# An attention with two mixtures of experts: first products by seven block products, second products in two groups, and an order set by a list scheduler

## The chip, the cores and the metric
The kernel runs on one core of a Trainium2 chip. The metric is the device time of one execution in microseconds; a median of several executions is compared. All inputs lie in the chip's memory at the start, and the output is written there.

## The reference
Local and pooled attention over 576 tokens (2 batches, 8 heads of 64) gives 1152 tokens of 512 values. A mixture of 8 experts, whose weights come from a gate normalized in 8 rounds over rows and columns, makes new tokens of them, and a second mixture of 4 experts, with given probabilities, makes the output.
```python
# attention: exp of scores less their maxima, windows of 7 keys, plus means over 4 tokens
x = attn_out.transpose(0, 2, 1, 3).reshape(1152, 512)
# first mixture: w1 (8, 512, 1024), w2 (8, 1024, 512)
P = np.exp(x @ w_gate - (x @ w_gate).max())
for _ in range(8):
    P /= P.sum(1, keepdims=True) + 1e-09
    P /= P.sum(0, keepdims=True) + 1e-09
    P *= N / E
for e in range(E):
    h = np.maximum(x @ w1[e], 0.0)
    out += P[:, e:e + 1] * (h @ w2[e])
# second mixture: the same with 4 experts on out, and p = domain_probs / their sums
```

## The kernel before
Every operand of a product is kept as two parts of the type fp32r, a high part (a rounded copy) and a low part (the rest). A product is three matmuls: high by high, high by low, low by high. Tokens are split like this in `xh` and `xl`, the hidden activations in `hh` and `hl`, the weights in `w1h`, `w1l`, `w2h`, `w2l`.

The attention goes over 8 pairs of heads (4 in each batch of 576 tokens) in a hand-written order. From pair 4 on, units of the first expert's first products for batch 0 (`filler`, 288 tokens by 128 hidden values, 12 matmuls) stand between its steps. The gate of the first mixture follows, its 8 rounds interleaved with the same units for batch 1.

Then the experts come one after the other. For the first products (`p1_in`, L128) an expert takes 8 tiles `f` of hidden values and 3 blocks of 384 tokens, 12 matmuls each (4 slices of the model dimension, three parts). `p1_out` makes the high part on ACT (L148) and the low part on DVE (L150). For the second products (`p2_in`, L164) it takes 9 tiles of 128 tokens, 24 matmuls of 512 columns each; `p2_out` scales them with the expert's probability and adds them into `acc` on DVE (L181). Weights are loaded in pieces of 128x512 into a ring of four buffers (`load_next`, SP's queue), and `split` makes the high part on ACT (L116) and the low part on POOL (L117), one piece per unit of products. Behind expert 7 `turn` transposes the result into new `xh` and `xl`. The order of all engines is the order in which the code is written.

## Time and profile before
| what | value |
|---|---|
| three runs | 1283.47, 1284.67 and 1288.3 us, median 1284.67 us |
| span of the profiled execution | 1281.9 us (its own time is not listed apart; 1.6 us below the quickest run) |
| busy: TensorE, weight loads, DVE, ACT, POOL | 1273.6, 1157.3, 319.6, 314.9, 289.4 us |
| chain that ended last, first and second products | 47% and 46% of the span |
| HBM traffic | 60.0 MB read, 49 GB/s |

The busy times of all engines overlap. A matmul's busy time includes its way through the array, so the distance between the starts of two matmuls in a row is what one costs. The chain of work that ended last is followed back from the last instruction to what released it.

### The profile page before, as it was taken

Reading aid. Unit: us, or ns where it says so; the run is one execution under the profiler, and the core shown is the slowest. Engines: PE = TensorE matmul, PEld = TensorE weight load, DVE = VectorE, ACT = ScalarE, POOL = GpSimd, SP = SyncE. Lnnn points to the kernel's source line nnn. Section 1 sums busy time; section 2 is a strip of 40 time slices with the busy share of each in tenths; the row PEclk is TensorE's granted clock in tenths of the full one; section 3 lists DMA queues with packets and bytes.
Section 4 is the critical chain, followed back from the end, with each engine's and each line's share of the span. In section 5 each row is a group of like instructions: output and inputs, shape, how many; then the busy total and the mean of one; then the engine's idle time right before and its main releaser. Section 6 shows DMA issues by size and latency. Waiting matters only on the chain.

```text
span 1281.9 us, 17529 instructions
## 1 busy us (share of the span) xinstructions
PE 1273.6 (99%) x7166; PEld 1157.3 (90%) x7166; DVE 319.6 (25%) x681; ACT 314.9 (25%) x758; POOL 289.4 (23%) x245
## 2 busy tenths in 40 slices
PE   9899999999999999999999999999999999999998
PEld 8799889889889989989989989989988988988987
DVE  6855202112112212212212212222200211211211
ACT  3653223203203303302302302312322320320310
POOL 5742222302402401401401311211221230230210
PEclk9899999999999999999999999999999999999999
DMA  7421111201301301200200210110111120120101
GB/s 199 137 64 48 54 38 43 89 1 42 91 1 36 97 1 34 84 16 27 81 25 25 63 45 22 46 49 25 46 45 42 42 82 1 47 86 1 34 26 50
DMA packets 33761, 63.52 MB, mean 50 GB/s; under 512 B 5280, under 2 KB 6048, under 8 KB 33680
## 3 DMA queue, kind: packets, MB, share of 16 engines
q1 hardware_dynamic: 33680, 62.40, 16.8%
q8 instruction: 56, 0.92, 0.3%
q14 instruction: 25, 0.20, 0.0%
HBM read 60.02 MB, written 2.36 MB: 49 GB/s over the span
## 4 chain that ended last, share of the span: by engine, by line
PE 97%; DVE 1%; ACT 0%; DMA 0%; issue 0%; ACTq 0%
PE bank L128 47%; PE bank L164 46%; PE bank L293 1%; PE bank L456 0%; PE bank L334 0%; PE bank L431 0%; DVE xl L491 0%; PE bank L192 0%; ACT ed L370 0%; DVE ed L400 0%; PE bank L739 0%; DMA qk<-in_qk_dram 0%; PE bank L464 0%; DVE mxd L348 0%; DVE sm L318 0%; PE bank L286 0%
## 5 line engine op out<-in xcount | busy, mean ns | idle before, releaser
L128 PE MATMUL bank<-xh,w1h 128*128 128x384 f32 (+1 forms) x1184 | 392.9, 332 | 0.0
L128 PE MATMUL bank<-xl,w1h 128*128 128x384 f32 (+1 forms) x1184 | 391.1, 330 | 0.0
L128 PE MATMUL bank<-xh,w1l 128*128 128x384 f32 (+1 forms) x1184 | 391.0, 330 | 0.0
L164 PE MATMUL bank<-w2h,hh 128*128 128x512 f32 (+1 forms) x872 | 339.9, 390 | 0.0
L164 PE MATMUL bank<-w2h,hl 128*128 128x512 f32 (+1 forms) x872 | 339.8, 390 | 0.0
L164 PE MATMUL bank<-w2l,hh 128*128 128x512 f32 (+1 forms) x872 | 337.4, 387 | 0.0
L148 ACT ACTIVATE hh<-bank 128x384 fp32r<-128x384 f32 (+5 forms) x392 | 148.9, 405 | 720.2 <-PE bank L128 685.9
L117 POOL TENSOR_TENSOR w2l<-stg,w2h 128x512 fp32r<-128x512 f32 x96 | 124.2, 1294 | 794.5 <-ACT w2h L116 794.5
L150 DVE SCALAR_TENSOR_TENSOR hl<-bank,hh 128x384 fp32r<-128x384 f32 (+5 forms) x392 | 168.1, 449 | 512.4 <-ACT hh L148 512.0
L128 PEld LDWEIGHTS bank<-xh,w1h 128*128 128x128 f32 x1184 | 222.8, 188 | 1.2 <-DVE sm L318 0.4
L128 PEld LDWEIGHTS bank<-xl,w1h 128*128 128x128 f32 x1184 | 222.9, 188 | 0.4
L128 PEld LDWEIGHTS bank<-xh,w1l 128*128 128x128 f32 x1184 | 222.8, 188 | 0.0
L164 PEld LDWEIGHTS bank<-w2l,hh 128*128 128x128 f32 x872 | 163.7, 188 | 34.9
L164 PEld LDWEIGHTS bank<-w2h,hh 128*128 128x128 f32 x872 | 163.8, 188 | 34.9
L164 PEld LDWEIGHTS bank<-w2h,hl 128*128 128x128 f32 x872 | 163.9, 188 | 32.1
L181 DVE SCALAR_TENSOR_TENSOR acc<-bank,prob,acc 128x512 f32<-128x512 f32 (+1 forms) x91 | 67.8, 745 | 416.7 <-PE bank L164 416.7
L117 POOL TENSOR_TENSOR w1l<-stg,w1h 128x512 fp32r<-128x512 f32 x96 | 122.6, 1300 | 115.9 <-ACT w1h L116 115.0
L116 ACT ACTIVATE w1h<-stg 128x512 fp32r<-128x512 f32 x96 | 58.2, 628 | 46.0 <-DMA stg<-in_w1a_dram 32.6
L116 ACT ACTIVATE w2h<-stg 128x512 fp32r<-128x512 f32 x96 | 59.8, 623 | 0.0
L179 ACT ACTIVATE acc<-bank,prob 128x512 f32<-128x512 f32 x18 | 12.4, 689 | 78.2 <-PE bank L164 66.4
L293 PEld LDWEIGHTS bank<-qk 64*64 64x64 f32 x288 | 21.2, 172 | 4.0 <-issue 2.9
L293 PE MATMUL bank<-qk 64*64 64x70 f32 x288 | 24.0, 271 | 0.2 <-DMA qk<-in_qk_dram 0.2
(94 smaller groups left out, 315.2 us busy)
## 6 DMA issues: line engine op xcount, KB each, us to landing
stg<-in_w1a_dram SPq DMA_DIRECT2D x64, 256.0 KB
stg<-in_w2a_dram SPq DMA_DIRECT2D x64, 256.0 KB
stg<-in_w1b_dram SPq DMA_DIRECT2D x32, 256.0 KB
stg<-in_w2b_dram SPq DMA_DIRECT2D x32, 256.0 KB
qk<-in_qk_dram SPq DMA_DIRECT2D x7, 576.0 KB
vw<-in_vw_dram SPq DMA_DIRECT2D x8, 315.0 KB
v<-in_v_dram SPq DMA_DIRECT2D x8, 288.0 KB
out_dram<-acc SPq DMA_DIRECT2D x8, 256.0 KB
```

Of the source, the lines that this page charges most:

```text
L116: nc.scalar.activation(out=hi, in_=t, func=ACTF.Copy)
L117: nc.gpsimd.tensor_tensor(out=lo, in0=t, in1=hi.bitcast(F32), op=ALU.subtract)
L128: nc.tensor.matmul(out=ps[:, 0:n], lhsT=a[f][:, k, :], rhs=b[:, k, t0:t0 + n], start=(k == 0 and p == 0), stop=(k == HP - 1 and p == 2),)
L148: nc.scalar.activation(out=hi, in_=ps[:, s:s + m], func=ACTF.Relu)
L150: nc.vector.scalar_tensor_tensor(out=lo, in0=ps[:, s:s + m], scalar=0.0, in1=hi.bitcast(F32), op0=ALU.max, op1=ALU.subtract,)
L164: nc.tensor.matmul(out=ps[:, 0:nd], lhsT=a[k][:, c:c + 128], rhs=b[k][:, c0:c0 + nd], start=(k == 0 and p == 0), stop=(k == NF - 1 and p = ...
L179: nc.scalar.activation(out=a, in_=ps, func=ACTF.Copy, scale=s)
L181: nc.vector.scalar_tensor_tensor(out=a, in0=ps, scalar=s, in1=a, op0=ALU.mult, op1=ALU.add)
L293: nc.tensor.matmul(out=sc[p0:p0 + 64, (t - lo) * W:(t - lo + 1) * W], lhsT=qk_t[p0:p0 + 64, 0, 64 * t:64 * t + 64], rhs=qk_t[p0:p0 + 64, 1 ...
```

## The change
The first products are made by Strassen's scheme. The two batches of 576 tokens and the two halves of the model dimension are the 2x2 blocks of one operand, the halves of the model dimension and two tiles of hidden values (`q` and `q` + 4, a *quarter*, 256 values) the blocks of the other. Seven products per quarter stand in place of eight: products 1, 2 and 4 use blocks of x, products 5, 6, 7 and 3 use sums of its blocks (`sh`, `sl`, made once per mixture by `x_sums` with POOL, DVE and ACT). Each product is made for two halves `u` of 288 tokens, 6 matmuls of 288 columns. `quad` makes the weights of the seven products, with four differences on POOL and seven splits. `quarter_products` puts the seven together in three pairs of banks, with additions on DVE and POOL in SBUF tensors (`p1`, `p5`, `u2`), from which `hidden` makes the parts of the activations.

The second products come after every two quarters (a *group*): nine tiles of 12 matmuls, with an accumulation each, so an expert has two. The hidden activations of one group (`ht`) are kept, not of a whole expert. The first group of experts 0 and 8 has its first products plain, in units of 288 tokens. In expert 0 the probability is multiplied in at the end.

All of it behind the attention is handed to `Plan` as tasks with an engine, a cost and what they read and write. `run` sets the order on each engine: of the first 48 tasks of an engine it takes the one that can begin first by its costs, with tasks of the gate ahead of all. In the attention the fillers are 8 units of first products and 8 halves of second products, and the loads for them go through `raw1` (one buffer of 128x1024) and `raw2` (two).

```diff
+class Plan:
+    AFTER = {"PE": 260.0, "ACT": 120.0, "DVE": 120.0, "POOL": 140.0, "DMA": 0.0}
+    LOOK = 48
...
+        def start(i):
+            e, cost, _, deps, bufs, _ = T[i]
+            t = free[e]
+            for d in deps:
+                if not done[d]:
+                    return None
+                t = max(t, end[d] + (0.0 if T[d][0] == e else self.AFTER[T[d][0]]))
...
+                if b.at != b.ring.given:
+                    return None
+                s = b.ring.free()
+                if s is None:
+                    return None
+                t = max(t, s[0] + 150.0)
+            return t
...
+    def load_first(j):
+        if j < 2:
+            nc.sync.dma_start(out=raw1[0].rearrange("p a b -> p (a b)"), in_=w1a[0, j])
...
+    def split_first(j):
+        if j < 4:
+            q, h = divmod(j, 2)
+            for b in (2 * h, 2 * h + 1):
+                t, w = raw1[0][:, b], w1s[4 * q + b]
+                nc.scalar.activation(out=w[:, 0], in_=t, func=ACTF.Copy)
+                nc.gpsimd.tensor_tensor(out=w[:, 1], in0=t, in1=w[:, 0].bitcast(F32), op=ALU.subtract)
+            if j == 1:
+                load_first(1)
...
-    nsplit = {3: 1, 4: 2, 5: 2, 6: 2, 7: 1}
+    nsplit = {3: 1, 4: 2, 5: 3, 6: 2}
...
+    raw1.append(late.tile([128, 4, 256], F32, name="raw1_1"))
...
+    r_w1, r_w2, r_raw1, r_raw2 = Ring(w1s), Ring(w2s), Ring(raw1), Ring(raw2)
+    r_t = Ring([late.tile([128, 256], F32, name=f"t_{j}") for j in range(3)])
+    r_tmp = Ring([late.tile([128, U], F32, name=f"tmp_{j}") for j in range(8)])
...
+    def split(ring, src, key, n):
+        b = ring.new()
+        plan.add("ACT", copy_cost(n), lambda: nc.scalar.activation(
+            out=b.slot[:, 0], in_=src(), func=ACTF.Copy), (key,), ((b, 0),))
+        plan.add("POOL", pool_cost(n), lambda: nc.gpsimd.tensor_tensor(
+            out=b.slot[:, 1], in0=src(), in1=b.slot[:, 0].bitcast(F32), op=ALU.subtract),
+            (key, (b, 0)), ((b, 1),))
+        return b
...
+    def quad(g, q):
+        r = load_quad(g, q)
...
+        def less(x, kx, y, ky):
+            t = r_t.new()
+            plan.add("POOL", pool_cost(256), lambda: nc.gpsimd.tensor_tensor(
+                out=t.slot, in0=x(), in1=y(), op=ALU.subtract), (kx, ky), (t,))
+            return lambda: t.slot, t
+        w = {1: split(r_w1, b11, r, 256)}
+        t1, k1 = less(b12, r, b11, r)
+        w[5] = split(r_w1, t1, k1, 256)
+        t2, k2 = less(b22, r, t1, k1)
+        w[6] = split(r_w1, t2, k2, 256)
+        w[2] = split(r_w1, b21, r, 256)
+        t3, k3 = less(b22, r, b12, r)
+        w[7] = split(r_w1, t3, k3, 256)
+        w[3] = split(r_w1, b22, r, 256)
+        t4, k4 = less(b21, r, t2, k2)
+        w[4] = split(r_w1, t4, k4, 256)
+        return w
...
+    def product(p, w, ps, u, first):
...
+            o = ps.slot[:, 0:U]
+            for k in range(2):
+                for n, (j, hl) in enumerate(((0, 0), (0, 1), (1, 0))):
+                    if kind == "x":
+                        c = i * S + u * U
+                        a = (xh, xl)[hl][:, rest[0] + k, c:c + U]
+                    else:
+                        a = (sh, sl)[hl][:, i, k, u * U:u * U + U]
+                    nc.tensor.matmul(
+                        out=o, lhsT=w.slot[:, j, 128 * k:128 * k + 128], rhs=a,
+                        start=(first and k == 0 and n == 0), stop=(k == 1 and n == 2),
+                        skip_group_check=True,
+                    )
+        plan.add("PE", 6 * 133.4, fn, [(w, 0), (w, 1), *keys], (ps,))
...
+    def add(dst, ps, b, cost=457.0):
+        plan.add("DVE", cost, lambda: nc.vector.tensor_tensor(
+            out=dst.slot, in0=ps.slot[:, 0:U], in1=b.slot, op=ALU.add), (ps, b), (dst,))
+    def quarter_products(w, q):
+        fa, fb = 2 * (q % 2), 2 * (q % 2) + 1
+        R = range(2)
+        X, p1 = [r_bank.new() for u in R], [r_tmp.new() for u in R]
+        for u in R:
+            product(1, w[1], X[u], u, True)
+            act_copy(lambda u=u: p1[u].slot, lambda u=u: X[u].slot[:, 0:U], 412.0, (X[u],), (p1[u],))
+        Z, p5 = [r_bank.new() for u in R], [r_tmp.new() for u in R]
+        for u in R:
+            product(5, w[5], Z[u], u, True)
+            act_copy(lambda u=u: p5[u].slot, lambda u=u: Z[u].slot[:, 0:U], 412.0, (Z[u],), (p5[u],))
+            plan.add("POOL", pool_cost(U), lambda u=u: nc.gpsimd.tensor_tensor(
+                out=p5[u].slot, in0=p5[u].slot, in1=p1[u].slot, op=ALU.add), (p1[u], p5[u]), (p5[u],))
+        Y, u2 = [r_bank.new() for u in R], [r_tmp.new() for u in R]
+        for u in R:
+            product(6, w[6], Y[u], u, True)
+            add(u2[u], Y[u], p1[u])
+        for u in R:
+            product(2, w[2], X[u], u, False)
+            hidden(lambda u=u: X[u].slot[:, 0:U], X[u], fa, 0, u, P_EVICT)
+        for u in R:
+            product(7, w[7], Y[u], u, False)
+            add(p5[u], Y[u], p5[u])
+            hidden(lambda u=u: p5[u].slot, p5[u], fb, 1, u, S_EVICT)
+        for u in R:
+            product(3, w[3], Z[u], u, False)
+            add(u2[u], Z[u], u2[u])
+            hidden(lambda u=u: u2[u].slot, u2[u], fb, 0, u, S_EVICT)
+        for u in R:
+            product(4, w[4], Y[u], u, False)
+            add(p1[u], Y[u], p1[u])
+            hidden(lambda u=u: p1[u].slot, p1[u], fa, 1, u, S_EVICT)
...
+    def x_sums(j):
...
+                t = part[b][h]
+                plan.add("POOL", pool_cost(2 * wd), lambda t=t, o=o, h=h: nc.gpsimd.tensor_tensor(
+                    out=v(t), in0=xh[:, 2 * h:2 * h + 2, o:o + wd].bitcast(F32),
+                    in1=xl[:, 2 * h:2 * h + 2, o:o + wd].bitcast(F32), op=ALU.add), keys, (t,))
+        def two(dst, x, y, op):
+            plan.add("DVE", dve_cost(2 * wd), lambda: nc.vector.tensor_tensor(
+                out=v(dst), in0=v(x), in1=v(y), op=op), (x, y), (dst,))
+        (a11, a12), (a21, a22) = part
+        two(a22, a21, a22, ALU.add)
+        two(a21, a11, a21, ALU.subtract)
+        two(a11, a22, a11, ALU.subtract)
+        two(a12, a12, a11, ALU.subtract)
+        for i, t in enumerate((a22, a11, a21, a12)):
+            hi, lo = sh[:, i, :, c:c + wd], sl[:, i, :, c:c + wd]
+            plan.add("ACT", copy_cost(2 * wd), lambda t=t, hi=hi: nc.scalar.activation(
+                out=hi, in_=v(t), func=ACTF.Copy), (t,), (("s", i, j, 0),))
+            plan.add("DVE", dve_cost(2 * wd), lambda t=t, hi=hi, lo=lo: nc.vector.tensor_tensor(
+                out=lo, in0=v(t), in1=hi.bitcast(F32), op=ALU.subtract),
+                (t, ("s", i, j, 0)), (("s", i, j, 1),))
...
+    def gate_round(it):
+        pc = r_bank.new()
+        gate("PE", 600.0, lambda: nc.tensor.matmul(
+            out=pc.slot[:, 0:ncol], lhsT=ones, rhs=prob1.rearrange("p n e -> p (n e)")), ("p",), (pc,))
...
+    first_w1 = [held(r_w1, j) for j in range(8)]
+    first_w2 = [held(r_w2, j) for j in range(4)]
+    gate_start()
+    plan.later = [(9000.0 + 4200.0 * it, lambda it=it: gate_round(it)) for it in range(8)]
+    for q in range(2):
+        for h in range(2):
+            for u in range(2):
+                plain_unit(first_w1[4 * q + 2 * h:4 * q + 2 * h + 2], 2 * q + h, 1, u)
+        for j in range(2):
+            x_sums(2 * q + j)
+    for n in range(4, NN):
+        accumulate(0, n, tile_products(first_w2, n), "copy")
+    for q in (2, 3):
+        quarter_products(quad(0, q), q)
+    w2_ = second(0, 1)
...
-    for g in range(NE):
-        last1 = g == E1 - 1
-        if g:
-            for f in range(NF):
-                for j, (t0, n) in enumerate(blocks):
...
-                    p1_group(f, t0, n)
-                split(g, 1, f)
...
+    for g in range(1, NE):
+        for grp in range(2):
+            if g == E1 and grp == 0:
+                ws = [plain_quad(g, q) for q in range(2)]
+                for b, u in T_OF:
+                    for q in range(2):
+                        for h in range(2):
+                            plain_unit(ws[q][2 * h:2 * h + 2], 2 * q + h, b, u)
+                            if (b, u, q, h) == (0, 0, 0, 1):
+                                turn(NN - 1)
+                for j in range(4):
+                    x_sums(j)
...
```

**TensorE in a later expert.** Before, two parts of one block of tokens (`w1h_102` and `w1l_110` are the weights of hidden tile 4; columns 384):
```order
L128 MATMUL bank_119<-xh,w1h_102 128x384
L128 MATMUL bank_119<-xl,w1h_102 128x384
L128 MATMUL bank_119<-xh,w1l_110 128x384
L128 MATMUL bank_119<-xh,w1h_102 128x384
L128 MATMUL bank_119<-xl,w1h_102 128x384
L128 MATMUL bank_119<-xh,w1l_110 128x384
```
Now, product 1 for both halves and the first matmuls of product 5 (`w1s_80`, `w1s_81` hold high and low part):
```order
L900 MATMUL bank_105<-xh,w1s_80 128x288
L900 MATMUL bank_105<-xl,w1s_80 128x288
L900 MATMUL bank_105<-xh,w1s_80 128x288 x2
L900 MATMUL bank_105<-xl,w1s_80 128x288
L900 MATMUL bank_105<-xh,w1s_80 128x288
L900 MATMUL bank_99<-xh,w1s_80 128x288
L900 MATMUL bank_99<-xl,w1s_80 128x288
L900 MATMUL bank_99<-xh,w1s_80 128x288 x2
L900 MATMUL bank_99<-xl,w1s_80 128x288
L900 MATMUL bank_99<-xh,w1s_80 128x288
L900 MATMUL bank_106<-sh,w1s_81 128x288
L900 MATMUL bank_106<-sl,w1s_81 128x288
```
A weight slot now serves 6 matmuls of 288 columns twice, and the moving operand changes from `xh`, `xl` to the sums `sh`, `sl`.

**TensorE at the gate's start** (L671 the logits' transposes, L687 the maxima's, L693 the broadcast). Before, from the logits' transposes on, with the rows of the units between left out:
```order
L128 MATMUL bank_118<-xh,w1l_106 128x288
L671 MATMUL bank_114<-ident,lg 128x16 x9
L128 MATMUL bank_119<-xh,w1h_98 128x288
L128 MATMUL bank_119<-xl,w1h_98 128x288
...
L128 MATMUL bank_120<-xh,w1l_107 128x288
L687 MATMUL bank_115<-ident,gm 1x128
L128 MATMUL bank_121<-xh,w1h_99 128x288
...
L128 MATMUL bank_121<-xh,w1l_107 128x288
L693 MATMUL bank_114<-gr,ones 128x1
```
Now (L1076, L1096 and L1102 are the same three):
```order
L319 MATMUL bank_101<-xl,wg_b 16x288
L1076 MATMUL bank_99<-ident,lg 128x16 x9
L1096 MATMUL bank_100<-ident,gm 1x128
L1102 MATMUL bank_101<-gr,ones 128x1
L265 MATMUL bank_102<-xh,w1s_80 128x288
L265 MATMUL bank_102<-xl,w1s_80 128x288
L265 MATMUL bank_102<-xh,w1s_80 128x288 x2
```
The three steps stand directly behind one another, and the units of batch 1 behind all of them.

**DVE in the gate's rounds.** Before, one round with the low parts of two units:
```order
L719 TENSOR_REDUCE cs<-bank_115 128x8
L723 RECIPROCAL cs<-cs 128x8
L724 SCALAR_TENSOR_TENSOR prob_74<-prob_74,cs 128x9x8
L701 TENSOR_REDUCE rs<-prob_74 128x9
L702 RECIPROCAL rs<-rs 128x9
L703 TENSOR_TENSOR prob_74<-prob_74,rs 128x9x8
L150 SCALAR_TENSOR_TENSOR hl_3_93<-bank_118,hh_3_85 128x64
L150 SCALAR_TENSOR_TENSOR hl_3_1463<-bank_118,hh_3_1455 128x224
L150 SCALAR_TENSOR_TENSOR hl_3_1463<-bank_119,hh_3_1455 128x288
```
Now, the sums of x for the later tokens (L1011; L1023 their low parts) begin behind a round and a low part of the hidden activations (L870), and another round stands among them:
```order
L870 SCALAR_TENSOR_TENSOR ht<-bank_102,ht 128x288
L1011 TENSOR_TENSOR tmp_1386<-tmp_1387,tmp_1386 128x288
L1114 TENSOR_REDUCE cs<-bank_100 128x8
L1118 RECIPROCAL cs<-cs 128x8
L1120 SCALAR_TENSOR_TENSOR prob_71<-prob_71,cs 128x9x8
L1063 TENSOR_REDUCE rs<-prob_71 128x9
L1066 RECIPROCAL rs<-rs 128x9
L1067 TENSOR_TENSOR prob_71<-prob_71,rs 128x9x8
L1011 TENSOR_TENSOR tmp_1387<-tmp_1388,tmp_1387 128x288
L1011 TENSOR_TENSOR tmp_1388<-tmp_1386,tmp_1388 128x288
L1011 TENSOR_TENSOR tmp_1385<-tmp_1385,tmp_1388 128x288
L1023 TENSOR_TENSOR sl<-tmp_1386,sh 128x2x144
```
The sums and their low parts share DVE's queue with the rounds, and both read two SBUF tensors in each row of L1011, L1023, L1067 and L1120.

## Rows read from the trace of the kernel before
**Rows 1.** The page: busy line of TensorE, and the chain by engine.
```profile
PE 1273.6 (99%) x7166; PEld 1157.3 (90%) x7166; DVE 319.6 (25%) x681; ACT 314.9 (25%) x758; POOL 289.4 (23%) x245
...
PE 97%; DVE 1%; ACT 0%; DMA 0%; issue 0%; ACTq 0%
```
**Rows 2.** The chain in order of time: start us, us, what.
```profile
99.37 3.17 PE bank L128 x24
...
110.37 1.60 PE bank L128 x12
...
332.23 49.24 PE bank L164 x216
381.47 49.94 PE bank L128 x288
```
**Rows 3.** TensorE, order of time, 288 columns: start us, us, engine, line, operation.
```profile
66.18 0.30 PE L128 MATMUL bank<-xl,w1h 128*128 128x288 f32 x1
...
69.10 0.30 PE L128 MATMUL bank<-xh,w1l 128*128 128x288 f32 x1
```
**Rows 4.** Busy us (instructions) of PE, PEld, DVE, ACT, POOL; clock, DMA, GB/s.
```profile
400.00:600.00 200.00, 200.00 (x1020) 182.64 (x1019) 41.88 (x83) 43.32 (x98) 41.13 (x33) 1.00 0.14 43
```
**Rows 5.** Groups by line and shape: count, busy us, mean ns, idle before.
```profile
L117 POOL TENSOR_TENSOR w2l<-stg,w2h 128x512 fp32r<-128x512 f32 x96 | 124.2, 1294 | 794.5 <-ACT w2h L116 794.5
...
L181 DVE SCALAR_TENSOR_TENSOR acc<-bank,prob,acc 128x512 f32<-128x512 f32 x89 | 66.8, 751 | 412.2 <-PE bank L164 412.2
...
L150 DVE SCALAR_TENSOR_TENSOR hl<-bank,hh 128x288 fp32r<-128x288 f32 x24 | 11.0, 457 | 21.3 <-ACT hh L148 21.2
...
L148 ACT ACTIVATE hh<-bank 128x288 fp32r<-128x288 f32 x24 | 9.9, 412 | 30.4 <-PE bank L128 30.4
...
L272 POOL TENSOR_TENSOR vd<-t 72x256 f32<-72x256 f32 x8 | 5.9, 734 | 0.6
```
**Rows 6.** Two lines of DVE alone: count, least/median/greatest ns, first and last start.
```profile
L491 DVE TENSOR_TENSOR xl<-xs,xh x8: 697/1305/1740, 33.5 to 99.8; 128x576 fp32r<-128x576 f32 x8
...
L724 DVE SCALAR_TENSOR_TENSOR prob<-prob,cs x8: 233/1068/1077, 117.0 to 145.4; 128x72 f32<-128x72 f32 x8
```
**Rows 7.** POOL and DVE in order of time, in the gate's rounds.
```profile
127.04 1.29 POOL L117 TENSOR_TENSOR w2l<-stg,w2h 128x512 fp32r<-128x512 f32 x1 [2.10 <-ACT w2h L116]
...
127.36 1.07 DVE L724 SCALAR_TENSOR_TENSOR prob<-prob,cs 128x72 f32<-128x72 f32 x1
...
139.12 0.24 DVE L719 TENSOR_REDUCE cs<-bank 128x8 f32<-128x80 f32 x1 [2.97 <-PE bank L712]
...
140.43 0.23 DVE L703 TENSOR_TENSOR prob<-prob,rs 128x72 f32<-128x72 f32 x1
```
**Rows 8.** DVE in order of time, at the gate's start.
```profile
107.94 0.30 DVE L679 COPY lg<-bank 128x144 f32<-128x144 f32 x1
108.34 0.23 DVE L682 TENSOR_TENSOR prob<-lg 128x72 f32<-128x72 f32 x1
...
111.24 0.27 DVE L690 TENSOR_REDUCE gr<-bank 1x1 f32<-1x128 f32 x1
```
**Rows 9.** TensorE in the attention, then a window as in rows 4.
```profile
55.45 0.31 PE L431 MATMUL bank<-ident,sm 128*70 128x128 f32 x1 [1.46 <-DVE xs L478]
...
61.99 0.44 PE L128 MATMUL bank<-xh,w1h 128*128 128x288 f32 x1
62.23 0.44 PE L128 MATMUL bank<-xl,w1h 128*128 128x288 f32 x1
...
58.00:60.00 2.00, 2.00 (x20) 1.62 (x19) 1.33 (x3) 2.00 (x6) 0.00 (x0) 0.50 0.05 12
```
**Rows 10.** First load (the chain), then POOL and ACT in the attention.
```profile
0.73 3.78 DMA qk<-in_qk_dram
...
60.36 2.51 POOL L117 TENSOR_TENSOR w1l<-stg,w1h 128x512 fp32r<-128x512 f32 x2 [2.44 <-ACT w1h L116]
...
64.30 0.41 ACT L148 ACTIVATE hh<-bank 128x288 fp32r<-128x288 f32 x1 [3.50 <-PE bank L128]
```

More of the change, by code (lines that the diff above doesn't have):

```diff
@@ L18, with __init__, new, free @@
 NEG = -1e30
-MAIN = (2, 2, 2, 2, 2, 0, 0, 0)
 HALVES = ((0, 5), (5, 9))
+class Buf:
+    def __init__(self, ring):
+        self.ring, self.slot, self.left, self.end, self.at = ring, None, 0, 0.0, ring.made
+        ring.made += 1
+class Ring:
+    def __init__(self, slots):
+        self.slots = list(slots)
+        self.owner = [None] * len(self.slots)
+        self.made = self.given = 0
+    def new(self):
+        return Buf(self)
+    def free(self):
+        best = None
+        for j, b in enumerate(self.owner):
+            if b is not None and b.left:
+                continue
+            t = b.end if b is not None else 0.0
+            if best is None or t < best[0]:
+                best = (t, j)
+        return best
@@ L91, in bank @@
         return banks[which[n % len(which)]]
-    staged = {}
-    order = []
-    for g in range(NE):
-        order += [(g, 0, f) for f in range(NF)] + [(g, 1, f) for f in range(NF)]
-    nxt = [0]
-    def load_next():
-        if nxt[0] >= len(order):
-            return
-        g, which, f = order[nxt[0]]
-        nxt[0] += 1
-        src = experts[g][which]
-        t = stg.tile([128, 512], F32, tag="stg", name="stg")
-        nc.sync.dma_start(out=t, in_=src[experts[g][2], f])
-        staged[g, which, f] = t
@@ new lines, in p1_plain, with h_high @@
+    def p1_plain(ps, slots, c, k0, k1):
+        for k in range(k0, k1):
+            w = slots[k // 2]
+            a = (k % 2) * 128
+            for p, (j, b) in enumerate(((0, xh), (0, xl), (1, xh))):
+                nc.tensor.matmul(
+                    out=ps[:, 0:U], lhsT=w[:, j, a:a + 128], rhs=b[:, k, c:c + U],
+                    start=(k == 0 and p == 0), stop=(k == HP - 1 and p == 2),
+                )
+    def h_high(ps, s, c):
+        nc.scalar.activation(out=ht[:, s, 0, c:c + U], in_=ps, func=ACTF.Relu)
@@ new lines, in h_low, with p2_part @@
+    def h_low(ps, s, c):
+        nc.vector.scalar_tensor_tensor(
+            out=ht[:, s, 1, c:c + U], in0=ps, scalar=0.0,
+            in1=ht[:, s, 0, c:c + U].bitcast(F32), op0=ALU.max, op1=ALU.subtract,
+        )
+    def p2_part(ps, n, slots, s0, first, last):
+        for j in range(2):
+            w = slots[j]
+            for p, (a, b) in enumerate(((0, 0), (1, 0), (0, 1))):
+                nc.tensor.matmul(
+                    out=ps, lhsT=ht[:, s0 + j, a, 128 * n:128 * n + 128], rhs=w[:, b, :],
+                    start=(first and j == 0 and p == 0), stop=(last and j == 1 and p == 2),
+                )
@@ L185, in logits, with filler @@
+    fill = [(fill_p1, q, h, u) for q in range(2) for h in range(2) for u in range(2)]
+    fill += [(fill_p2, n, half) for n in range(4) for half in range(2)]
+    def filler(n):
+        for _ in range(min(n, len(fill))):
+            f, *args = fill.pop(0)
+            f(*args)
     def logits(b):
-        n = S // 2
-        for t0 in (b * S, b * S + n):
+        for t0 in (b * S, b * S + U):
             ps = bank()
@@ L609, in tile_attention_moe_moe @@
         if i == HP - 2:
-            for _ in range(4):
-                load_next()
+            for j in (0, 2, 3):
+                load_first(j)
         pool_v(i + 1)
@@ new lines, in turn, with fn, src @@
+    def turn(n):
+        ps = r_bank.new()
+        def fn():
+            for k in range(HP):
+                nc.tensor.transpose(
+                    ps.slot[:, k * 128:(k + 1) * 128], acc[n][:, k * 128:(k + 1) * 128], ident
+                )
+        plan.add("PE", 4 * 260.0, fn, (("acc", n),), (ps,))
+        hi, lo = (x[:, :, 128 * n:128 * n + 128] for x in (xh, xl))
+        def src():
+            return ps.slot.rearrange("p (k t) -> p k t", k=HP)
+        plan.add("ACT", 600.0, lambda: nc.scalar.activation(
+            out=hi, in_=src(), func=ACTF.Copy), (ps,), (("x", n), ("xh", n)))
+        plan.add("DVE", 691.0, lambda: nc.vector.tensor_tensor(
+            out=lo, in0=src(), in1=hi.bitcast(F32), op=ALU.subtract), (ps, ("xh", n)), (("x", n),))
@@ L782, in _layout @@
+    plan.run()
 def _layout(inputs):
```

507 lines of the change are left out of this document (312 added, 195 removed).

## The prediction
> **What bounds the kernel now.** I read the busy line first: TensorE is busy 99% of the span and the chain that ended last is 97% TensorE [rows 1]. The chain in order of time shows why: behind 183 us it is made of whole experts, 288 matmuls of the first products in 49.94 us and 216 of the second in 49.24 us, with no wait between [rows 2]. That is 173.4 ns for 384 columns and 228.0 ns for 512, so a matmul costs its columns at 2.4 GHz (160.0 and 213.3 ns) and 13 to 15 ns more. The other engines are far from full there: in 200 us DVE 41.9, ACT 43.3, POOL 41.1 [rows 4]. So time comes off only by taking matmuls from TensorE, and is given back only where DVE, ACT or POOL then make it wait.
>
> **First products: what is taken away.** Before there are 3168 matmuls of 384 columns and 384 of 288; the changed program has 4080 of 288 columns and none of 384 (336 in each of ten experts, 360 in experts 0 and 8). The pitch at 288 columns is in the trace: 22 matmuls from 66.18 to 69.10 us, 132.7 ns [rows 3], with 132.1 and 133.3 ns in two pieces of the chain [rows 2]. Per expert 336 × 132.7 ns = 44.6 us against 49.94, 5.3 us less, ten times 53.5 us. Expert 0 loses 24 matmuls (3.2 us), expert 8 goes to 360 × 132.7 ns = 47.8 us (2.2 us). Sum **-58.9 us** (-61.3 at 132.1 ns, -56.6 at 133.3). An eighth of the columns would be 63.4 us at 2.4 GHz; the rest is lost to 528 more matmuls, each with its fixed 12 ns.
>
> The Trainium skill, "TensorE: Matmul & The Clock Gate", section "Back-to-back issue gap", gives N/2.4 + 2.5 ns, 162.5 ns at 384 and 122.5 ns at 288 columns. By it an expert would save 5.6 us and the sum would be some 3 us larger. The rows say 173.4 and 132.7 ns for this data type, and I go by them.
>
> **Second products** stay 9 × 24 matmuls of 512 columns per expert, now in two groups of 12 per tile: 0 on TensorE. The second group costs 108 more accumulations of 0.75 us on DVE [rows 5], one per 2.74 us of matmuls; they lie beside those.
>
> **New work beside TensorE, in a normal group** (two quarters of 84 matmuls, 11.1 us each, then nine tiles, 24.6 us). DVE per quarter: 10 operations that read a bank at 0.457 us [rows 5] and 6 low halves that read two SBUF tensors. The latter price is not in the trace at 288 columns: between L724's quickest (72 columns, 0.233 us) and L491's (576 columns, 0.697 us) [rows 6] a straight line gives 0.43 us. So 7.2 us in 11.1 us. ACT: 8 evictions and 4 copies at 0.412 us [rows 5] and some 8 weight copies, under 9 us. POOL per group: 22 weight operations of 256 columns at 0.73 us, 4 of 512 at 1.29 us [rows 5], 4 additions at 0.73 us: 24.2 us of 46.9.
>
> DVE and POOL do not run free of one another, though. L724 takes 0.233 us alone and 1.07 us when it begins inside a POOL subtraction: begun at 127.36, it ends at 128.43, and POOL's operation that began at 127.04 ends at 128.33 [rows 7]. L491 spreads from 0.697 to 1.740 us [rows 6]. Both read two SBUF tensors. So each such operation can wait for the rest of a POOL operation, on average half of 0.73 us: DVE's quarter grows from 7.2 to 9.4 us, and to 11.5 us if each waits for a whole one, which is 0.4 us more than the quarter, and the tiles (DVE 6.8 us of 24.6) take up that backlog.
>
> The Trainium skill, "SBUF — State Buffer", section "Who interferes with whom", states the rule: a DVE instruction with two SBUF inputs and a GpSimd instruction that reads SBUF exclude each other for a whole instruction. The trace agrees at L724 (0.233 against 1.07 us). By it POOL too is held up, and that side is the last rival below.
>
> The tightest chain in a quarter is POOL's addition into `p5`. A bank is read some 0.2 us behind its last pitch (a matmul is 0.30 us long [rows 3]), so ACT's two copies end 3.1 and 3.9 us into the quarter, the two additions at 3.9 and 4.7 at the earliest, and DVE wants them when product 7 ends, at 7.4 and 7.9. Between one pair of additions and the next POOL has 10 operations of 0.73 us and one of 1.29 us, with the pair 10.1 of 11.1 us; 6 DVE low halves in between make it 12.7, so 1.6 us late, and 3.2 us are there. I take 0.1 us per group, **+2 us** over 22 groups (0 to 22).
>
> **Around the first expert** the cover is thinner, and I see four waits.
> - TensorE's order now holds the gate's start in one piece: nine transposes of the logits, the transpose of the maxima, the broadcast, and only then a unit of products. Before, 12 to 24 matmuls stood between. DVE's 0.30, 0.23 and 0.23 us and 0.27 us [rows 8], the wait for the last copy of the logits (0.45 us) and some six hand-overs now stand bare: **+2.5 us** (1.5 to 4).
> - The sums of x. TensorE reaches product 5 of the later tokens 30.6 us after it begins (8 units of 1.59 us, 5 tiles of 2.74, 24 matmuls, 7 matmuls of the gate). DVE's order has its first sum behind the evictions of two units, 4.3 us in; then up to the needed row 29 operations on two SBUF tensors (12.5 us), 6 evictions (2.7) and 6 rounds of the gate of 1.54 us each (139.12 to 140.66 us [rows 7], 9.2): 28.7 us, no wait at all. But POOL has 26 operations of 0.74 us in these 31 us, so is busy 60% of them, and 41 operations of DVE (two in each round) can meet one: with 0.22 us each it is 37.7 us, with 0.37 us 43.9. I take the middle, **+7 us** (0 to 13).
> - DVE then still has 9 to 12 us of work for a quarter of which TensorE has 8 us left: **+2 us** (0 to 5).
> - The clock: behind a stretch of small matmuls with an idle time of 1.46 us in it TensorE ran at the lower level, 1.2 GHz (granted 0.50 from 58 to 60 us, and at 62 us its matmuls were 0.24 us apart) [rows 9]. A wait of 7 us may do this once, for some 12 matmuls that then take 0.11 us more each: **+1.5 us** (0 to 4).
>
> **In the attention** the same number of fillers runs, but `raw1` has one buffer: pair 4 splits its second half and asks for the next load at once. ACT then waits for POOL's two subtractions (60.4 to 61.9 us) and a load of 512 KB, longer than the first load of the page, 3.78 us [rows 10], so to some 66.6 us. ACT was idle 3.5 us there before [rows 10]; the third filler needs the first one's bank and waits: **+1 us** (0 to 4).
>
> **Sum.** -58.9 + 2 + 2.5 + 7 + 2 + 1.5 + 1 = -42.9 us. The profiled execution spans 1281.9 us; the three runs are 1283.5 to 1288.3, their median 2.8 us above that span. Against the span this is 1239.0 us, with the 2.8 us **1242 us** (1284.67 - 42.9 = 1241.8).
>
> **Rivals.**
> - *No waits around the first expert*: POOL and DVE rarely meet, the sums are ready at 28.7 us. 1284.7 - 58.9 + 4 = 1230 us. For it: they meet only where POOL runs at that moment, and DVE's order is static while POOL itself waits for DVE's buffers; against: POOL is asked for 60% of that stretch.
> - *The queues lag in every group.* ACT's order mixes weight copies that wait for POOL with evictions; a POOL late by 1 us more than its cover holds back ACT, then DVE, then product 4. 1 us per group gives 1242 + 22 = 1264 us, 2 us gives 1286. For it: 12.7 us asked of an 11.1 us quarter. Against: tiles of 24.6 us empty the queues after every second quarter.
> - *Slower: POOL and DVE become the bound.* If POOL's 24.2 us and DVE's 12 × 0.43 us all fell into the two quarters, 29.4 us would be asked of 22.3, 7.1 us too much in each of 22 groups: 1242 + 156 = 1398 us. It decides from 2.2 us per group on (1242 + 48 = 1290). Against: 12 weight slots for 14 products of a group let POOL work some 19 us ahead, through the tiles.
> - That matmuls at 288 columns are held by their weight loads is shut out by the pitch, 132.7 ns.
>
> **How the numbers follow.** My forecast has 0.60 and its own range 1232 to 1252; no waits 0.12; lag in every group 0.21, half of it below 1264; bound by POOL and DVE 0.05; 0.02 for what I don't see. The range 1228 to 1264 holds the first two and half of the third. A measurement of this kernel tells about 0.5%, 6.4 us, from no change: faster 0.93, within it 0.02, slower 0.05.
>
> **What would show it.** Right: products at 132 to 134 ns, an expert in some 94 us of chain; TensorE's idle time under 25 us, most of it between 100 and 170 us, ended by DVE's low halves of the sums; low halves on two SBUF tensors at 0.6 to 0.9 us on average. Wrong: idle time of 1 us or more in each group, ended by DVE or ACT behind POOL's additions; a granted clock of 0.5 outside the attention and the first expert; a pitch above 135 ns.

## The result and the profile after

The changed kernel takes 1243.55 us (median of four runs, 1241.95 to 1249.04) against 1286.49 us (also four runs; the three known at the prediction had 1284.67), a ratio of 0.9677 with a 95% interval of 0.9645 to 0.9708. The forecast was 1242 us. The profiled execution took 1241.95 us and spans 1240.2 us, 41.7 us less than the 1281.9 us of before; the sum had said 42.9 less.

The page, the busy line of TensorE and the chain by engine, as in [rows 1]:

```profile
PE 1220.9 (98%) x7682; PEld 1096.6 (88%) x7682; DVE 654.6 (53%) x1197; ACT 467.0 (38%) x1195; POOL 660.6 (53%) x769
...
PE 93%; DVE 4%; DMA 1%; ACT 1%; issue 1%; POOL 0%; SPq 0%; POOLq 0%; DVEq 0%; ACTq 0%
```

TensorE still bounds the kernel, but 4% of the chain is DVE's. The other 93% are read from the chain in order of time, as in [rows 2] (L900 are the seven products, L959 the second products):

```profile
193.38 22.27 PE bank L900 x168
215.65 24.96 PE bank L959 x108
240.61 22.26 PE bank L900 x168
262.87 24.52 PE bank L959 x108
```

No wait stands between these pieces, nor in the groups behind them. A group's products take 22.27 us, 132.5 ns each (the pitch, from the start of one matmul to the start of the next). The second products show what the forecast didn't have: 24.96 us in two groups of three, 24.52 us in every third, where a half of the 216 before took 24.62 us.

Windows: busy us (instructions) of PE, PEld, DVE, ACT, POOL, then clock, DMA share, GB/s:

```profile
106.70:110.10 3.40, 3.40 (x15) 3.40 (x15) 1.00 (x4) 0.57 (x2) 2.11 (x4) 0.50 0.03 5
110.10:113.50 3.40, 3.40 (x27) 3.40 (x27) 1.79 (x5) 0.87 (x3) 0.00 (x0) 1.00 0.00 0
127.20:130.60 3.40, 3.40 (x10) 2.62 (x9) 3.13 (x10) 0.00 (x0) 3.40 (x5) 0.50 0.00 0
106.60:153.00 46.40, 40.01 (x227) 35.62 (x227) 39.94 (x89) 21.69 (x55) 34.45 (x42) 0.93 0.13 46
...
400.00:600.00 200.00, 200.00 (x1171) 180.68 (x1170) 103.50 (x179) 70.35 (x178) 111.80 (x130) 1.00 0.13 47
```

From 400 to 600 us DVE is at 103.5 and POOL at 111.8 of 200 us, beside a TensorE that never waits ([rows 4] had 41.9 and 41.1). Around the first expert DVE is busy 39.9 of 46.4 us, and TensorE waits. TensorE's rows there, idle time and its releaser in brackets (L1076 transposes of the logits, L1096 of the maxima, L1102 the broadcast, L1112 the rounds of the gate; the last row is the second expert's first matmul):

```profile
103.40 0.29 PE L1076 MATMUL bank<-ident,lg 16*128 16x16 f32 x2
...
105.69 0.27 PE L1096 MATMUL bank<-ident,gm 128*1 128x128 f32 x1 [1.32 <-DVE gm L1093]
106.33 0.38 PE L1102 MATMUL bank<-gr,ones 1*128 1x1 f32 x2 [0.37 <-DVE gr L1098]
...
126.09 0.46 PE L1112 MATMUL bank<-prob,ones 128*128 128x90 f32 x2 [3.09 <-DVE prob L1067]
...
146.94 0.40 PE L900 MATMUL bank<-sl,w1s 128*128 128x288 f32 x1 [1.35 <-DVE sl L1023]
...
152.68 0.46 PE L1112 MATMUL bank<-prob,ones 128*128 128x90 f32 x2 [1.41 <-DVE prob L1067]
...
193.22 0.30 PE L900 MATMUL bank<-xh,w1s 128*128 128x288 f32 x1
```

Two rounds of the gate wait for DVE, 3.09 and 1.41 us, and a product waits for a sum of x, 1.35 us (two more waits there are 0.22 and 0.32 us). What DVE did in that stretch (groups of lines: count, busy us, mean ns, idle before):

```profile
L1023 DVE TENSOR_TENSOR sl<-tmp,sh 128x288 fp32r<-128x288 f32 x16 | 11.7, 768 | 0.0
L1011 DVE TENSOR_TENSOR tmp<-tmp,tmp 128x288 f32<-128x288 f32 x16 | 11.3, 708 | 0.3
L1067 DVE TENSOR_TENSOR prob<-prob,rs 128x72 f32<-128x72 f32 x8 | 4.3, 540 | 0.3
...
L1120 DVE SCALAR_TENSOR_TENSOR prob<-prob,cs 128x72 f32<-128x72 f32 x7 | 3.5, 500 | 0.2
```

These 47 operations all read two SBUF tensors and took 30.8 us. At their quickest (0.45 us for 288 columns, 0.24 for 72) they would take 18.0 us. Where the rest goes, two pairs show, DVE and POOL in order of time:

```profile
118.52 0.77 POOL L807 TENSOR_TENSOR w1s<-t,w1s 128x256 fp32r<-128x256 f32 x1
118.60 1.00 DVE L1023 TENSOR_TENSOR sl<-tmp,sh 128x288 fp32r<-128x288 f32 x1
...
144.38 0.74 POOL L831 TENSOR_TENSOR t<-raw,t 128x256 f32<-128x256 f32 x1
144.41 1.03 DVE L1011 TENSOR_TENSOR tmp<-tmp,tmp 128x288 f32<-128x288 f32 x1
```

DVE's operation ends 0.31 and 0.32 us behind the end of the POOL operation that ran when it began (119.60 against 119.29, 145.44 against 145.12). The same holds for the low halves of the hidden values in the groups (least/median/greatest ns), of which the form that reads a bank never spreads:

```profile
L870 DVE SCALAR_TENSOR_TENSOR ht<-tmp,ht x264: 440/627/1582, 155.4 to 1215.4; 128x288 fp32r<-128x288 f32 x132
L870 DVE SCALAR_TENSOR_TENSOR ht<-bank,ht x112: 439/457/459, 110.3 to 1207.6; 128x288 fp32r<-128x288 f32 x112
```

Of the 252 behind 190 us, 234 begin inside a POOL operation, and 93% of those end 0.313 to 0.320 us behind its end.

### The profile page after: what moved, and what is told of

It reads as the page before. It is cut to its first block, busy times and chain, and to the rows that moved or that the text cites. A ratio compares the mean times of both kernels' runs of the same rounds, so it can differ in the third digit from the quotient of the medians.

```text
span 1240.2 us, 19888 instructions
## 1 busy us (share of the span) xinstructions
PE 1220.9 (98%) x7682; PEld 1096.6 (88%) x7682; DVE 654.6 (53%) x1197; ACT 467.0 (38%) x1195; POOL 660.6 (53%) x769
## 4 chain that ended last, share of the span: by engine, by line
PE 93%; DVE 4%; DMA 1%; ACT 1%; issue 1%; POOL 0%; SPq 0%; POOLq 0%; DVEq 0%; ACTq 0%
PE bank L959 46%; PE bank L900 39%; PE bank L265 4%; DMA qk<-in_qk_dram 1%; DVE tmp L1011 1%; PE bank L420 1%; PE bank L558 1%; DVE sl L1023 1%; PE bank L284 1%; PE bank L583 0%; PE bank L551 0%; PE bank L1033 0%; DVE prob L1067 0%; DMA raw<-in_w2a_dram 0%; DMA raw<-in_w1a_dram 0%
## 5 line engine op out<-in xcount | busy, mean ns | idle before, releaser
L959 PE MATMUL bank<-w2s,ht 128*128 128x512 f32 x2556 | 593.4, 392 | 0.0
L959 PEld LDWEIGHTS bank<-w2s,ht 128*128 128x128 f32 x2556 | 477.3, 188 | 104.6
L900 PE MATMUL bank<-sh,w1s 128*128 128x288 f32 x1408 | 294.7, 295 | 0.0
L900 PEld LDWEIGHTS bank<-sh,w1s 128*128 128x128 f32 x1408 | 230.8, 188 | 0.1
L900 PE MATMUL bank<-xh,w1s 128*128 128x288 f32 x1056 | 228.2, 295 | 0.3 <-ACT tmp L798 0.3
L910 DVE TENSOR_TENSOR tmp<-bank,tmp 128x288 f32<-128x288 f32 x352 | 158.1, 451 | 132.3 <-ACT w1s L805 93.8
L900 PE MATMUL bank<-sl,w1s 128*128 128x288 f32 x704 | 207.8, 295 | 1.3 <-DVE sl L1023 1.3
L870 DVE SCALAR_TENSOR_TENSOR ht<-tmp,ht 128x288 fp32r<-128x288 f32 x264 | 202.6, 779 | 7.0 <-ACT ht L868 6.6
L900 PEld LDWEIGHTS bank<-xh,w1s 128*128 128x128 f32 x1056 | 175.6, 188 | 1.4 <-ACT tmp L798 0.6
L900 PE MATMUL bank<-xl,w1s 128*128 128x288 f32 x528 | 155.9, 295 | 0.0
L900 PEld LDWEIGHTS bank<-sl,w1s 128*128 128x128 f32 x704 | 132.2, 188 | 1.6 <-DVE sl L1023 1.6
L900 PEld LDWEIGHTS bank<-xl,w1s 128*128 128x128 f32 x528 | 99.1, 188 | 0.9
```

The lines of the kernel that those rows point to most:

```text
L870: plan.add("DVE", c0[1], lambda: nc.vector.scalar_tensor_tensor(out=ht[:, s, 1, c:c + U], in0=src(), scalar=0.0, in1=ht[:, s, 0, c:c + U]. ...
L900: nc.tensor.matmul(out=o, lhsT=w.slot[:, j, 128 * k:128 * k + 128], rhs=a, start=(first and k == 0 and n == 0), stop=(k == 1 and n == 2), ...
L910: plan.add("DVE", cost, lambda: nc.vector.tensor_tensor(out=dst.slot, in0=ps.slot[:, 0:U], in1=b.slot, op=ALU.add), (ps, b), (dst,))
L959: nc.tensor.matmul(out=ps.slot[:, 0:nd], lhsT=ht[:, j, a, 128 * n:128 * n + 128], rhs=w[j].slot[:, b, c0:c0 + nd], start=(j == 0 and p == ...
```

## The experiments

Executions of one program differ in the attention, whose instructions are the same in every kernel here: the transposes of the logits begin at 103.4 to 110.5 us. So, beside the median, each kernel has two stretches of its profiled execution: A from the transposes of the logits to the second expert's first matmul (above 103.40 to 193.22, 89.82 us), B from there to the end of the last matmul.

| kernel | median us | ratio to before (95%) | transposes begin | A | B |
|---|---|---|---|---|---|
| changed | 1243.55 | 0.9677 (0.9645 to 0.9708) | 103.40 | 89.82 | 1043.67 |
| all plain | 1302.39 | 1.0152 (1.0126 to 1.0177) | 103.42 | 83.27 | 1110.58 |
| first expert plain | 1240.90 | 0.9664 (0.9638 to 0.9689) | 104.66 | 84.87 | 1043.72 |
| ring of four | 1234.49 | 0.9615 (0.9595 to 0.9636) | 106.17 | 85.51 | 1036.95 |
| gate mixed | 1241.85 | 0.9682 (0.9655 to 0.9710) | 110.17 | 88.41 | 1043.67 |
| four, rounds late | 1237.29 | 0.9633 (0.9610 to 0.9655) | 109.10 | 86.82 | 1036.94 |
| four, first plain | 1232.55 | 0.9598 (0.9580 to 0.9616) | 106.02 | 83.01 | 1037.02 |
| four, turned | 1231.93 | 0.9601 (0.9578 to 0.9625) | 103.37 | 85.39 | 1036.96 |
| more on POOL | 1249.80 | 0.9727 (0.9706 to 0.9749) | 109.34 | 91.80 | 1043.67 |
| three edits | 1229.14 | 0.9561 (0.9542 to 0.9580) | 108.54 | 80.28 | 1037.02 |
| late buffers (one run) | 1247.66 | | 110.45 | 90.59 | 1041.53 |
| changed, again | 1244.22 | 0.9677 (0.9660 to 0.9693) | 107.65 | 90.92 | 1043.67 |

**All plain.** All groups use plain units, and there are no sums of x:

```diff
...
-                for q in (2 * grp, 2 * grp + 1):
-                    quarter_products(quad(g, q), q)
+                ws = [plain_quad(g, q) for q in (2 * grp, 2 * grp + 1)]
+                for b, u in T_OF:
+                    for q in range(2):
+                        for h in range(2):
+                            plain_unit(ws[q][2 * h:2 * h + 2], 2 * q + h, b, u)
```

> Every group's first products are plain: 192 matmuls of 288 columns in place of 168, in all 22 groups that used seven products, with no sums of x and no additions behind the products; planner, second products and gate stay as in the changed kernel. Theory A (the gain is the seven products alone, and the rest of the change costs what the trace after shows): 22 x 24 x 132.55 ns = 70.0 us more matmuls, and the waits around the first expert (6.4 us of idle time and some 1.7 us of lower clock from 120 to 153 us) go with the sums: 1243.5 + 70.0 - 8.1 = 1305 us, 1302 to 1314. Theory B (the order by the planner, not the products, carries part of the gain): under 1290 us. A normal group must show 192 matmuls in 25.5 us in place of 168 in 22.27 us.

Theory A, and 1.5% slower than before: without the seven products the rest of the change is no gain. The chain of that kernel (L265 are its plain products):

```profile
237.28 25.44 PE bank L265 x192
262.72 24.50 PE bank L959 x108
```

Stretch B grows by 66.91 us, 21 groups of 3.19 us, and stretch A falls by 6.55 us although it has 3.18 us more of matmuls: the sums of x and what they bring cost 9.7 us there. The pattern of 24.96, 24.96 and 24.50 us in the second products is still there, so it has nothing to do with the products beside it.

**First expert plain.** Only the first expert's second group is plain, with its four sums of x behind it:

```diff
-        for j in range(2):
-            x_sums(2 * q + j)
...
-    for q in (2, 3):
-        quarter_products(quad(0, q), q)
+    ws = [plain_quad(0, q) for q in (2, 3)]
...
+    for j in range(4):
+        x_sums(j)
```

> Only the first expert's second group has plain products, and the sums of x stand behind them in the program; all else is the changed kernel. Theory A (the sums of x fill DVE while the gate's rounds and product 5 wait for it): 24 more matmuls of 132.55 ns cost 3.2 us, the idle time of 6.4 us between 120 and 153 us and the low clock of 127.1 to 130.5 us (1.7 us) go: 1243.5 + 3.2 - 8.1 = 1238.6 us. Theory B (the gate's rounds are late by their own chain, whatever DVE does beside them): the sums' own waits of 1.7 us go alone, 1243.5 + 3.2 - 1.7 = 1245 us, and an idle time of some 3 us ahead of a round stays.

Theory A: stretch A is 4.95 us shorter with 3.18 us more of matmuls, 8.1 us as forecast, and one wait of 0.9 us ahead of a round is left of 4.7:

```profile
PE bank L1112 <- DVE prob L1067: 0.9, 1, 0.9
```

The medians, 1240.90 and 1243.55 us, can't be told apart; the stretches are what shows it.

**Ring of four**, the kernel without the two later weight buffers:

```diff
-    w2s += [late.tile([128, 2, DM], F32R, name=f"w2s_{j}") for j in range(4, 6)]
```

> The ring of second-product weight buffers has the first four buffers, not six. In the trace after, a group that reads buffers 0 to 3 takes 24.52 us for its 108 matmuls (227.0 ns), the two groups out of three that read buffers 4 and 5 besides take 24.96 us (231.1 ns). Theory A (which buffers are read sets the pitch): all groups at 227.0 ns, some 15 groups x 0.44 us = 6.6 us less, 1237 us. Theory B (what else runs in these groups sets the pitch, and it comes back every third group): the pattern of three stays, 1243 us. Theory C (four buffers are too few: a group's weights then wait for the tiles before them to end): TensorE waits ahead of the tiles, slower than 1243 us; against it, 22.3 us of products lie between.

Theory A. Its chain (the line numbers are one lower):

```profile
260.87 24.52 PE bank L958 x108
285.39 22.27 PE bank L899 x168
307.66 24.52 PE bank L958 x108
```

Every group is at 227.0 ns, and stretch B is 6.72 us shorter, 15 groups of 0.45 us. Stretch A fell too, by 4.3 us, which no theory had: POOL's splits of second weights now come behind the first group's tiles, and the waits of 1.35, 1.41 and 0.32 us are gone. The wait of 3.1 us ahead of a round is not. In the changed kernel two of these splits met four operations of DVE:

```profile
135.56 2.54 POOL L807 TENSOR_TENSOR w2s<-raw,w2s 128x512 fp32r<-128x512 f32 x2
135.56 1.39 DVE L1067 TENSOR_TENSOR prob<-prob,rs 128x72 f32<-128x72 f32 x1
136.87 2.53 DVE L1011 TENSOR_TENSOR tmp<-tmp,tmp 128x288 f32<-128x288 f32 x3
```

In the ring of four the same four operations run without them and are 2.25 us shorter:

```profile
138.34 0.23 DVE L1066 TENSOR_TENSOR prob<-prob,rs 128x72 f32<-128x72 f32 x1
138.49 1.44 DVE L1010 TENSOR_TENSOR tmp<-tmp,tmp 128x288 f32<-128x288 f32 x3
```

**Four, turned.** The ring of four, where hidden slices 0 and 1 meet buffers 2 and 3 and the reverse:

```diff
-        for q in (2 * grp, 2 * grp + 1):
+        qs = (2 * grp, 2 * grp + 1)
+        turned = (g, grp) == (0, 1)
+        for q in reversed(qs) if turned else qs:
...
-        return out_
+        return out_[2:] + out_[:2] if turned else out_
```

> Four second-product buffers, but from the first expert's second group on the hidden slices 0 and 1 meet buffers 2 and 3, and slices 2 and 3 meet buffers 0 and 1; nothing else differs from the run with the ring of four. Theory A (the pitch of 231.1 ns comes from buffers 4 and 5 lying elsewhere): all tiles at 227.0 ns, 1234.5 us. Theory B (it comes from which hidden slice a weight buffer is paired with: in the trace after only the groups with buffer j at slice j were quick): 231.1 ns in 22 groups of 23, 22 x 0.44 us = 9.7 us more, 1244 us.

Theory A: the pitch stays at 227.0 ns, and stretch B with it. Which slice meets which buffer plays no part.

**Late buffers.** Second products from the first expert's second group on read four buffers in one row, the first two at the place of 4 and 5:

```diff
...
+    r_w2 = Ring(w2s[4:8])
```

> From the first expert's second group on, second products read four weight buffers that lie in one row behind each other, the first two of them where buffers 4 and 5 of the changed kernel lie; buffers 0 to 3 serve only the first group. To make room the planner has one buffer for loads of first weights in place of two, and 11 in place of 12 for their split halves. Theory A (the place of buffers 4 and 5 sets the pitch): 231 ns or more in all groups. Theory B (a group that reads buffers from two places is slow, each place by itself is quick): 227.0 ns in all groups. The total tells less, since the fewer buffers for first weights may make TensorE wait: 1237 us by B if they don't, 1247 by A.

Neither: 24.74 us in every group, 229.0 ns.

```profile
223.49 24.74 PE bank L959 x108
...
270.49 24.73 PE bank L959 x108
```

So the mean pitch of a group goes with the buffers that it reads: 227.0 ns for 0 to 3, 229.0 for the later four, 231.1 for a mix.

It is not the price of a single buffer. Read from the starts of the single matmuls, an unbroken group in the ring of four begins with six or eight pitches of 224 to 236 ns and then stays at 226 and 227. In a mixed group of the changed kernel the pitches go on between 224 and 240 ns to the end, also where the weights lie in buffers 0 to 3: each of the four slices has 228.8 ns or more on average. In the later four buffers they go round 226, 229 and 232. So the buffers decide whether the stream of matmuls settles at 227 ns; why is open.

**Gate mixed.** One unit of products between the transposes of the logits and of the maxima:

```diff
-    gate_start()
+    gate_start(lambda: unit(0))
...
+        between()
         pg = r_bank.new()
...
```

> One unit of 12 products (1.59 us) stands in TensorE's order between the nine transposes of the logits and the transpose of the maxima; all else as in the changed kernel. Theory A (the bare gate start costs its idle time and the lower clock behind it): the idle 1.32 us ahead of the maxima's transpose is covered, 0.37 us ahead of the broadcast stays, and the clock does not fall at 106.7 us, where 14 matmuls took 0.24 in place of 0.13 us: 1.3 + 1.4 = 2.7 us less, 1240.8 us. Theory B (the idle time only moves, since the rounds of the gate and the sums on DVE set the time until 153 us): the gap at 104.4 us goes, the waits at 123 and 151 us grow by as much, 1243 us.

Between the two theories. The gap of 1.32 us and the lower clock at the gate's start are gone, but the waits behind grow, and the clock is at its lower level around the first of them instead (129.2 to 136.1 us, as long as the two stretches of the changed kernel together):

```profile
131.57 0.73 PE L1113 MATMUL bank<-prob,ones 128*128 128x90 f32 x2 [4.62 <-DVE prob L1067]
...
140.18 0.46 PE L1113 MATMUL bank<-prob,ones 128*128 128x90 f32 x2 [1.10 <-DVE ht L870]
```

Stretch A is 1.41 us shorter, and the median can't be told from the changed kernel's.

**Four, rounds late:**

```diff
...
-    plan.later = [(9000.0 + 4200.0 * it, lambda it=it: gate_round(it)) for it in range(8)]
+    plan.later = [(28000.0 + 4200.0 * it, lambda it=it: gate_round(it)) for it in range(8)]
```

> Four second-product buffers as in the run with the ring of four (1234.5 us), and the gate's eight rounds begin behind 28 us of TensorE's work, not behind 9, with the same 4.2 us between them. The stretch from the transposes of the logits to the second expert was 85.51 us there, with a wait of 3.11 us ahead of the third round, one of 0.22 and 1.7 us of lower clock behind them. Theory A (rounds and sums of x compete for DVE in the same 25 us): these 5.0 us go, 80.5 us in that stretch, 1229.5 us. Theory B (the rounds then compete with the products' evictions, and the wait only moves): a wait of 2 us or more stands at a later round or product, 84 us or more, 1233 to 1236 us.

Theory B, with a median a little above its range: the wait stands at a product (behind an addition of DVE) and at a round.

```profile
152.65 0.61 PE L899 MATMUL bank<-xh,w1s 128*128 128x288 f32 x1 [2.65 <-DVE tmp L909]
...
169.09 0.46 PE L1111 MATMUL bank<-prob,ones 128*128 128x90 f32 x2 [1.26 <-DVE prob L1066]
```

**More on POOL:**

```diff
+    def more():
+        plan.add("POOL", pool_cost(U), lambda: nc.gpsimd.tensor_tensor(
+            out=junk, in0=junk, in1=junk, op=ALU.subtract), ("junk",), ("junk",))
...
```

It is called behind products 2, 7 and 3 of each quarter and half.

> The changed kernel with 12 additional operations of 288 columns on POOL in each of the 22 groups of seven products, six per quarter, behind products 2, 7 and 3; nothing reads what they write. 12 x 0.82 us = 9.8 us more on POOL per group, which is busy some 27 of 47.2 us now. Theory A (the 12 weight buffers let POOL work ahead through the tiles, so that there is cover of more than 10 us): no idle time of TensorE in the groups, 1243.5 us. Theory B (the lag in every group, the rival of the prediction): POOL asks 22 us and more of the 22.3 us of two quarters, its additions come late, and TensorE waits 1 to 5 us in each group, 1265 to 1350 us. DVE's low halves on two SBUF tensors, 0.78 us on average, must grow with POOL's busy share if the two take turns.

Theory A: stretch B is 1043.67 us, the same to 0.01 us, with POOL at 147.8 of 200 us.

```profile
400.00:600.00 200.00, 200.00 (x1196) 182.23 (x1196) 98.91 (x184) 74.80 (x190) 147.75 (x183) 1.00 0.13 44
```

Its profiled execution is longer by what lies ahead: transposes at 109.34 us, and 2 us in stretch A, where the clock was at its lower level for 13.7 us (6.8 in the changed kernel). The last sentence of the expectation failed: DVE's low halves took 0.70 us on average, not more than 0.78. In the changed kernel 234 of 252 met a running POOL operation already, 40 of them one of 512 columns (these 40 took 1.36 us on average); here 9 met such a one. In the ring of four none did, and the average is 0.69 us with POOL as busy as in the changed kernel. What counts is which POOL operation runs, not how busy POOL is.

**Four, first plain**, both edits:

> Four second-product buffers, and the first expert's second group with plain products, its sums of x behind them. If the two edits add up, the stretch from the transposes of the logits to the second expert is 84.87 us, as with the plain group alone, less 0.45 us for the pitch of one group's tiles, 84.4 us, and the rest 1037.0 us as with the ring of four: 1233.4 us. That is 1 us less than the ring of four alone, since the 3.2 us of more matmuls nearly eat the 4 us of waits. Theory B (the plain group needs the two further buffers): a wait ahead of its tiles, above 1236 us.

They more than add up: stretch A is 83.01 us against the 84.4 expected, and no wait of a round or a product is left in it.

**Three edits**, the gate mixed too:

> Three edits together: four second-product buffers, plain products in the first expert's second group with the sums of x behind them, and one unit of products between the transposes of the logits and that of the maxima. The run with the first two had 83.01 us from the transposes of the logits to the second expert, with a bare 1.25 us and 14 matmuls at the lower clock (1.4 us) at the gate's start. Theory A (without sums beside the rounds nothing is there that could take the place of that wait): 2.7 us less, 80.3 us, and 1037.0 us behind it: 1229.9 us. Theory B (as with the third edit alone, half of it comes back as a wait ahead of a round): 81.7 us, 1231.2 us.

Theory A, 80.28 us against 80.3, and 1229.1 against 1229.9. What TensorE still waits for behind 100 us is the broadcast:

```profile
PE bank L1102 <- DVE gr L1098: 0.4, 1, 0.4
```

This version beats both kernels, by 4.4% and 1.2%.

**Changed, again:**

> The changed kernel once more, for what differs between two executions of the same program. If the differences lie in the attention alone, as the traces so far say (its transposes of the logits begin at 103.4 to 110.2 us in kernels whose instructions up to there are the same), the stretch from there to the second expert is 89.8 us and that from there to the last matmul 1043.7 us, both within 0.3 us, while the first is anywhere from 103 to 110 us; the median then lies at 1241 to 1247 us. If the waits around the first expert come and go, 89.8 us does not come back.

Stretch B came back exactly. Stretch A was 1.1 us longer. The waits are there again and are 1.3 us more in all (0.81 in place of 0.22 us ahead of a round, and 0.68 us ahead of a second product). The clock was at its lower level for 6.8 us as in the first execution, but in one piece behind the gate's start (109.7 to 116.5): it did not fall behind the wait of 3.10 us this time. So stretch A holds to about 1 us, not to 0.3, and differences of 1 us in that column show nothing.

```profile
PE bank L1112 <- DVE prob L1067: 5.3, 3, 3.1
...
PE bank L900 <- DVE sl L1023: 1.3, 1, 1.3
...
PE bank L959 <- DVE ht L870: 0.7, 1, 0.7
```

## Why the prediction was right

The total was right within 1.2 us of span. The largest term was right, and most of the waits lie in the stretch that was named; that the sum came so near is in part luck. The second products and the clock cost 4.7 and 1.6 us more than forecast, and the normal groups and the sums of x cost 2 and 2.6 us less.

- *First products, -58.9 us*: right. An expert takes 44.54 us against 49.94, ten times 5.40; with expert 0 (3.2) and expert 8 (47.9 us against 50.15) it is 59.5 us. The plain kernel shows the same per group from the other side. The larger saving by the Trainium skill ("TensorE: Matmul & The Clock Gate", section "Back-to-back issue gap") did not come: 132.5 ns at 288 columns, where its formula, given there for an isolated matmul, yields 122.5. Two slips in the working change nothing: at 132.1 ns the term is 61.1, not 61.3 us, and 528 matmuls at 12 ns would be 6.3 us, where the 4.5 us between 63.4 and 58.9 are lost.
- *Second products, 0*: the mis-sized term. It cost +4.7 us: 16 groups of 24.96 and 7 of 24.52 us against 24.62. The ring of four needs 6.7 us less than the changed kernel, so its pitch lies below that of before. The forecast counted matmuls and took over their pitch of [rows 2]; it did not ask which buffers they read.
- *Normal groups, +2*: 0. The additions into `p5` never delay TensorE, and the run with 9.8 us more on POOL shows cover of more than that. The rival of a lag in every group (0.21) did not come: the 21 groups behind the first expert show not one wait.
- *Sums of x and DVE's backlog, +7 and +2*: 6.4 us of idle time between 120 and 153 us (3.09, 0.22, 0.32, 1.35, 1.41). The size was near (9 were forecast), the place right only in part. Product 5 waited 1.35 us; most came where a round of the gate stood behind sums in DVE's order. That sums and rounds fight for DVE is shown by the first expert plain (8.1 us gone), and that moving the rounds alone doesn't help by the late rounds. That POOL's operations hold DVE up there (30.8 us in place of 18.0) the trace shows. The ring of four moved two of them away, and waits of 3.1 us in all went with them; that nothing else of that edit ended these waits is not shown, and for the wait of 3.09 us POOL's part was not tried.
- *Gate's start, +2.5*: transposes to the first unit take 3.24 us. Before it was 6.04 us (106.17 to 112.21) with 36 matmuls of 0.1327 us in between, so 1.26 without: +2.0 us.
- *Clock, +1.5*: 3.1 us, since the clock fell twice, behind the gate's start and behind the wait of 3.09 us. 15 matmuls in 3.40 us where the next 3.40 us have 27 is 1.5 us; eight second products at 0.427 in place of 0.231 us are 1.6.
- *Attention, +1*: the transposes begin 2.77 us earlier than before, with 3.3 us less of fillers: +0.5 us. The wait that was forecast is in the trace: ACT waits for the second load through `raw1`, evicts a bank late, and TensorE waits 1.21 us. The plain kernel's execution has no such wait. The term is smaller than what the attention varies by, and a second buffer was not tried.

```profile
65.01 0.72 ACT L248 ACTIVATE w1s<-raw 128x256 fp32r<-128x256 f32 x2 [4.81 <-DMA raw<-in_w1a_dram]
...
66.58 0.40 PE L265 MATMUL bank<-xh,w1s 128*128 128x288 f32 x1 [1.21 <-DVE ht L274]
```

Together -59.5 + 4.7 + 0 + 6.4 + 2.0 + 3.1 + 0.5 = -42.8 us; measured were -41.7, so 1.1 us are left over.

The low halves' 0.78 us on average lay in the forecast's 0.6 to 0.9. The rule of the Trainium skill that was weighed there ("SBUF — State Buffer", section "Who interferes with whom") is borne out by the trace: an operation that takes 0.45 us alone ends 0.31 us behind the end of the POOL operation that it met.

## What to carry to other kernels

Where one engine bounds and its order is kept full, a saving of its instructions arrives whole, and the others can more than double their work unseen. What is given back comes at places where a chain of small steps (here the gate) shares a second engine with a burst of new work; it is cheaper to do such a place the plain way (here 3.2 us of matmuls for 8.1 us of waits and lower clock) than to reorder it. And compare the time of the same instruction group by group: a period of three in 22 equal groups pointed to a ring of buffers and to the 6.7 us that one deleted line brought.
